# Moving the third batch's loads ahead of the second pass's W1, and the first batch's beta split behind the fourth pair's q

## The chip, the cores and the metric

The kernel runs on one core of a Trainium2 chip. The metric is the device time of one execution in microseconds (us), lower is better. One execution was also taken with the hardware profiler; all rows below come from it.

## The reference

For each of 8 batches, grouped-query attention runs over 384 positions (16 query heads, 4 key/value heads, head size 64), and its result, laid out as 384 x 1024, goes through an affine token-mixing and channel-mixing block:

```python
attn = softmax(q @ k.T / sqrt(64)) @ v        # per head; 4 q heads share a k, v head
x    = attn.transpose(0, 2, 1, 3).reshape(8, 384, 1024)
a1   = alpha1 * x + beta1
u    = x + lam * einsum('ts,bsd->btd', w_tok, a1)
a2   = alpha2 * u + beta2
out  = u + lam * (relu(a2 @ w_ch1) @ w_ch2)   # w_ch1 1024 x 4096, w_ch2 4096 x 1024
```

## The kernel before, in words

`main(b)` is the channel mixing of batch b and is called a pass here; there are eight. Its first half is `h` (line 407): 32 groups of 8 matmuls each, whose 256-column tiles of W1 come from HBM again in every pass through a ring of five (`load_w1`, line 128, on the POOL queue). Its second half is `ch` (line 441): two column halves times three row blocks, each 32 matmuls against W2, which is loaded once, during the first pass, and stays (`load_w2`, line 133, POOL queue).

`side(b)` is the attention and token mixing of batch b. For batches 1 to 7 its steps are woven, one at a time, between the matmuls of the pass before: `main(b)` yields after each four matmuls, and the loop at the end of the kernel compares the work done (`t` against `t_all`) with the share of steps issued. For the first batch no pass is there to hide it: its steps run alone at the start, in an order written out by hand (the dictionary `at`: after the scores of step i, the listed functions are issued). Every engine takes its instructions in the order in which these functions issue them.

The functions that matter at the start, with their lines: `scores` (202, exponent on ACT at 211), `av_piece` (237 on PE; then on DVE reciprocal 242, x 243, product with alpha1 247), `q_transpose` (188, copied out at 190), `k_transpose` (177, 179), `wtok_transpose` (297, copied out on DVE at 300), `rows_r` (307 and 311 on PE, 314 on ACT, 315 to 317 on DVE), `tok` (259, 263; DVE 266). In batch 0 lam is folded into alpha1 and beta1, and beta enters as one more product of rank 32 (line 263): `scale_rows(1)` (519) multiplies the beta1 rows by lam, `split(1, 2)` (527, 528, 527, 528, 531) writes them as a sum of bf16 rows in `rows_b`, `fill_h` (535) spreads them into `H`, and `tok` needs `H` and `R` (from `rows_r`). Buffers of PSUM are shared by tags: `av`, one of the q transposes and `tok` of batch 0 take turns in the two buffers of the tag `mm`; `wtok_transpose` and others in the one buffer each of `av` and `tp`.

The loads of batch b+2 happen in pass b: `load_k` at its start on the SP queue, later `place_k` (four casts on POOL, line 101), `load_q` (110) and `load_v` (105) on the POOL queue, and then `flip_k` and `flip_q` (113, 117), two DMA transposes on the SP queue, which also carries the stores of `out` (448) and the transposes of `a2` (282). In the first pass the POOL queue also holds, at the end of `h`, the five W1 tiles of the second pass.

Of the kernel before, what the change touches and what calls it, by code (L numbers as in the profile page):

```python
# [12 lines left out]
def kernel(  # L13
# [29 lines left out]
    B, Hq, S, D = q.shape  # L43
# [37 lines left out]
    def by_st(ap):  # L81
        return ap.rearrange("h (p st) d -> p st h d", st=NST)
# [3 lines left out]
    def load_k(b, hs=(0, 2)):  # L86
        ks.setdefault(b, [])
        for h in hs:
            t = sb.tile([P, 2, NST, D], f32, tag="kst", name="kst", bufs=2)
            nc.sync.dma_start(out=t, in_=k[b, h:h + 2].rearrange("h (p st) d -> p h st d", st=NST))  # L90
            ks[b].append(t)

    def place_k(b, i, hs=(0, 1)):
        if b not in k2s:
            k2s[b] = sb.tile([P, NST, Hkv, 2, D], bf, tag="k2", name="k2", bufs=1)
        copies = [nc.gpsimd.tensor_copy] * 2
        if b == 1 or b == 0 == i:
            copies = (nc.vector.tensor_copy, nc.vector.tensor_copy if i else nc.scalar.copy)
        lo, hi = hs[0], hs[-1] + 1
        for a in range(2):  # L100
            copies[a](out=k2s[b][:, :, 2 * i + lo:2 * i + hi, a, :], in_=ks[b][i][:, lo:hi].rearrange("p h st d -> p st h d"))

    def load_v(b, sts=range(NST)):
        for st in sts:
            nc.gpsimd.dma_start(out=vt[b % 2][:, st, :, :D], in_=by_st(v[b])[:, st])

    def load_q(b):
        qrs[b] = sb.tile([P, Hq, NST, D], bf, tag="q_raw", name="q_raw", bufs=1)
        for h in range(0, Hq, G):
            nc.gpsimd.dma_start(out=qrs[b][:, h:h + G], in_=q[b, h:h + G].rearrange("h (p st) d -> p h st d", st=NST))  # L110

    def flip_k(b):
        nc.sync.dma_start_transpose(out=kT.rearrange("p st h s -> p (st h) s"),
                                    in_=k2s[b].rearrange("p st h a d -> p (st h a d)"))

    def flip_q(b):
        nc.sync.dma_start_transpose(out=qT.rearrange("p a j s -> p (a j) s"),
                                    in_=qrs[b].rearrange("p h st d -> p (h st d)"))
# [5 lines left out]
    def load_w1(n):  # L124
        if n < B * NCH:
            t = sb.tile([P, NDT, CW * P], bf, tag="w1", name="w1", bufs=RING)
            c = n % NCH
            nc.gpsimd.dma_start(out=t, in_=w1src[:, :, c * CW * P:(c + 1) * CW * P])  # L128
            w1_tiles[n] = t

    def load_w2(dw, i, n):
        r, cs = slice(i * NNT // n, (i + 1) * NNT // n), slice(dw * 512, (dw + 1) * 512)
        nc.gpsimd.dma_start(out=w2[:, r, cs], in_=w2src[:, r, cs])
# [6 lines left out]
    def evac(eng):  # L140
        return nc.scalar.copy if eng == "ACT" else nc.vector.tensor_copy
# [16 lines left out]
    def side(b):  # L158
# [173 lines left out]
        def add(f, *a):  # L332
            us.append(lambda: f(*a))
# [35 lines left out]
        lower, upper = range(NP // 2), range(NP // 2, NP)  # L369
        def av(p):  # L370
# [2 lines left out]

        ut = a2_transpose
        at = {0: [(warmup, 3), (scale_rows, 0), (split, 0, 1, 0)], 1: [(k_transpose, 1, 1), (split, 0, 1, 1)],
              2: [(q_transpose, 2, 2, "av")], 3: [(warmup, 1), (spread, lower, (0, 1), "tp"), (scale_rows, 1), (split, 1, 2, 0)],
              4: [(split, 1, 2, 1), (av, 0)], 5: [(wtok_transpose, 0, "av"), (wtok_transpose, 1, "tp")],
              6: [(av, 1), (wtok_transpose, 2, "av"), (k_transpose, 2, 2, "tp")], 7: [(q_transpose, 4, 2, "av"), (fill_h, 0)],
              8: [(rows_r, "tp"), (av, 2)], 9: [(spread, upper, (0, 1), "av", "ACT"), (q_transpose, 6, 2, "mm")],
              10: [(tok, 0)],  # L380
              11: [(av, 3)], 12: [(tok, 1), (ut, 0)], 13: [(av, 4), (tok, 2)], 14: [(ut, 1), (fill_h, 4), (tok, 3)],
              15: [(av, 5), (ut, 2)], 16: [(tok, 4), (ut, 3)], 17: [(av, 6), (tok, 5)]}
# [4 lines left out]
        for f, *a in ((ut, 4), (h_part, (0, 1), range(4)), (av, 7), (ut, 5), (tok, 6),  # L387
                      (h_part, (2, 3), range(4)), (h_part, range(4), (4,)), (ut, 6), (tok, 7),
                      (h_part, range(4), (5,)), (ut, 7), (h_part, range(4), (6,)), (h_part, range(4), (7,))):
            add(f, *a)  # L390
        return us


    T_H, T_C = 4 * S, 4 * 512

    def main(b):
        a2T = a2Ts[b % 2]
        x = xs.pop(b)
        n = S + 1 if b == 0 else S
        for c in range(NCH):  # L400
            w1 = w1_tiles.pop(b * NCH + c)
            for j in range(CW):
                nt = c * CW + j
                begun = b == 0 and nt in early
                ps = early[nt] if begun else psum.tile([P, 512], f32, tag="mm", name="h", bufs=2)
                for dt in range(0 if begun else NDT):
                    nc.tensor.matmul(out=ps[:, :n], lhsT=w1[:, dt, j * P:(j + 1) * P],  # L407
                                     rhs=a2T[:, dt, :n], start=(dt == 0), stop=(dt == NDT - 1))
                    if dt == 3:
                        yield T_H  # L410
                c1 = bias1[:, nt:nt + 1]
                if b == 0:
                    evac("DVE" if nt % 2 else "ACT")(out=c1, in_=ps[:, S:n])
                if nt % 2 == 0:
                    nc.scalar.activation(out=hT[:, nt, :], in_=ps[:, :S], func=RELU, bias=c1)  # L415
                else:
                    nc.vector.tensor_scalar(out=hT[:, nt, :], in0=ps[:, :S], scalar1=c1,  # L417
                                            scalar2=0.0, op0=ADD, op1=mybir.AluOpType.max)
                yield T_H

            if b or c + RING < NCH:
                load_w1(b * NCH + c + RING)
            if b == 0 and c in (3, 5, 7, 9):
                load_w2(0, 8 + c // 2 - 1, 16)
            if b == 0 and c == NCH - RING:
                for i in (6, 7):
                    load_w2(0, i, 8)
                for i in range(8):
                    load_w2(1, i, 8)
            if b == 0 and c == NCH - 1:  # L430
                for i in range(RING):
                    load_w1(NCH + i)
        for dw in range(NDW):
            cs = slice(dw * 512, (dw + 1) * 512)
            for ms in range(NST):
                ps = psum.tile([P, 512], f32, tag="mm", name="ch", bufs=2)
                o = sb.tile([P, 512], f32, tag="tmp", name="o", bufs=4)
                last = (b, dw, ms) == (B - 1, NDW - 1, NST - 1)
                for lo, hi in ((0, 256), (256, 384), (384, 512)) if last else ((0, 512),):
                    for nt in range(NNT):  # L440
                        nc.tensor.matmul(out=ps[:, lo:hi], lhsT=hT[:, nt, ms * P:(ms + 1) * P],  # L441
                                         rhs=w2[:, nt, dw * 512 + lo:dw * 512 + hi], start=(nt == 0), stop=(nt == NNT - 1))
                        if nt % 4 == 3 and nt < NNT - 1:
                            yield T_C
                    c = slice(dw * 512 + lo, dw * 512 + hi)
                    nc.vector.tensor_tensor(out=o[:, lo:hi], in0=ps[:, lo:hi], in1=lam_t[:, c], op=MUL)  # L446
                    nc.vector.tensor_tensor(out=o[:, lo:hi], in0=o[:, lo:hi], in1=x[:, ms, c], op=ADD)  # L447
                    nc.sync.dma_start(out=out[b].rearrange("(p st) d -> p st d", st=NST)[:, ms, c], in_=o[:, lo:hi])
                yield T_C

    t_all = 2 * NNT * T_H + 8 * NST * NDW * T_C
    order = {mybir.EngineType.PE, mybir.EngineType.DVE, mybir.EngineType.Activation,
             mybir.EngineType.Pool, mybir.EngineType.SP}
    with tc.manual_schedule(engines=order):
# [97 lines left out]
        for f in side(0):  # L552
            f()
        place_k(1, 0)
        place_k(1, 1)
        for b in range(B):
            us = side(b + 1) if b + 1 < B else []
            half = False
            done, t, loaded, flipped = 0, 0, b + 2 >= B, b + 2 >= B
            lead, span = (0.04, 0.82) if b == 0 else (0, 0.95)  # L560
            if not loaded:
                load_k(b + 2)
            for dt in main(b):
                t += dt
                half = not half
                if late and half:
                    late.pop(0)()
                if done < len(us) and done * t_all * span < len(us) * (t - t_all * lead):
                    us[done]()
                    done += 1  # L570
                if not loaded and t > t_all * 0.55:
                    loaded = True
                    place_k(b + 2, 0)
                    place_k(b + 2, 1)
                    load_q(b + 2)
                    load_v(b + 2)
                if not flipped and t > t_all * 0.85:
                    flipped = True
                    flip_k(b + 2)
                    flip_q(b + 2)  # L580
            while done < len(us):
                us[done]()
                done += 1
# [30 lines left out]
```

## Time and profile before

| | |
|---|---|
| median of 6 runs | 813.1 us (812.38 to 814.86) |
| the profiled execution | 813.11 us, of it span 811.0 us |
| PE busy | 800.7 us (99% of the span) |
| DVE, ACT, POOL busy | 344.4, 225.9, 178.1 us |
| mean granted TensorE clock | 0.998 |
| bytes | 112.96 MB in DMA packets, mean 139 GB/s |
| first batch's attention alone | until about 41.7 us |
| first pass, `h` then `ch` | to 88.9 us, then to 138.5 us |
| each later pass but the last | 97.45 us |

Busy times are unions of an engine's instructions; matmuls overlap one another, so the mean duration of one is longer than its share of the time. A number in square brackets at the end of a timeline row is the time that the engine sat idle before it, and who ended it.

### The profile page before, as it was taken

What the parts mean: (1) busy time and instruction counts of PE and PEld (TensorE: products, weight loads), DVE (VectorE), ACT (ScalarE), POOL (GpSimd) and SP (SyncE); (2) the same over time, 40 slices, a digit from 0 to 9 for tenths busy, and PEclk for the clock granted to TensorE, in tenths of its full rate; (3) what the DMA queues carried; (4) which work ended last, traced back from release to release, by engine and by line L of the source; (5) the groups of instructions that cost most, each with busy time, mean ns of one, the idle gap of its engine ahead of it and who ended that gap; (6) DMA issues with size and microseconds to landing.
All of it is one profiled execution on the core that took longest, in us unless ns stands there. A gap on an engine that the chain in (4) does not pass through costs nothing.

```text
span 811.0 us, 14160 instructions
## 1 busy us (share of the span) xinstructions
PE 800.7 (99%) x6129; PEld 450.7 (56%) x6129; DVE 344.4 (42%) x669; ACT 225.9 (28%) x311; POOL 178.1 (22%) x232
## 2 busy tenths in 40 slices
PE   7999999999999999999999999999999999999997
PEld 4766555665556655566455655556555565556545
DVE  7745543244433444344452445434444344432122
ACT  5654311332113311233103331034211432102100
POOL 7135230334003230133202240022500321003000
PEclk9999999999999999999999999999999999999999
DMA  9999999999179992799848998499935998129611
GB/s 191 198 185 200 204 206 180 172 173 169 37 141 176 170 152 66 135 173 172 115 100 133 179 171 88 108 142 166 190 64 109 156 177 116 39 66 185 86 40 40
DMA packets 233550, 112.96 MB, mean 139 GB/s; under 512 B 82952, under 2 KB 227344, under 8 KB 233488
## 3 DMA queue, kind: packets, MB, share of 16 engines
q0 software_dynamic: 170736, 83.47, 83.7%
q1 hardware_dynamic: 62208, 28.20, 14.7%
q8 instruction: 48, 0.79, 0.4%
q10 hardware_dynamic: 544, 0.39, 0.1%
q14 instruction: 14, 0.11, 0.1%
HBM read 170.53 MB, written 12.58 MB: 226 GB/s over the span
## 4 chain that ended last, share of the span: by engine, by line
PE 95%; DVE 4%; issue 0%; ACT 0%; DVEq 0%
PE ch L441 41%; PE h L407 39%; PE av L237 4%; PE sc L202 4%; PE tok L259 4%; DVE hT L417 1%; DVE x L243 1%; PE h L152 1%; DVE a1f L250 0%; DVE a L252 0%; PE warm L459 0%; PE tp L188 0%; PE ut L276 0%; DVE hT L528 0%; PE vec L325 0%
## 5 line engine op out<-in xcount | busy, mean ns | idle before, releaser
L441 PE MATMUL ch<-w,hT 128*128 128x512 bf16 (+2 forms) x1600 | 353.4, 371 | 0.9 <-DVE o L446 0.9
L407 PE MATMUL h<-a2T,w 128*128 128x384 bf16 (+1 forms) x2016 | 349.5, 326 | 0.9 <-DVE hT L417 0.3
L407 PEld LDWEIGHTS <-w 128*128 128x128 bf16 x2016 | 189.4, 98 | 125.5 <-issue 8.7
L441 PEld LDWEIGHTS <-hT 128*128 128x128 bf16 x1600 | 146.3, 98 | 154.2 <-issue 5.8
L128 POOL DMA_DIRECT2D w<-in_moe_w_ch_dram x128 | 112.6, 882 | 541.1 <-PE h L407 493.7
L211 ACT ACTIVATE es<-sc 128x1024 bf16<-128x1024 f32 x126 | 123.4, 1021 | 289.2 <-PE sc L202 289.2
L417 DVE TENSOR_SCALAR hT<-h,bias 128x384 bf16<-128x384 f32 x128 | 79.0, 618 | 187.0 <-PE h L407 186.4
L415 ACT ACTIVATE hT<-h,bias 128x384 bf16<-128x384 f32 x128 | 74.3, 581 | 202.9 <-PE h L407 202.4
L446 DVE TENSOR_TENSOR o<-ch,vecs 128x512 f32<-128x512 f32 (+2 forms) x50 | 33.3, 667 | 91.1 <-PE ch L441 91.1
L266 DVE TENSOR_TENSOR x<-tok,x 128x384 f32<-128x384 f32 x64 | 35.6, 555 | 80.5 <-PE tok L259 78.3
L237 PEld LDWEIGHTS <-es 128*128 128x128 bf16 x1008 | 45.8, 97 | 20.5
L237 PE MATMUL av<-v,es 128*128 128x65 bf16 x1008 | 49.0, 193 | 0.0
L202 PE MATMUL sc<-qT,kT 64*128 64x384 bf16 (+2 forms) x576 | 46.0, 274 | 0.1
L259 PEld LDWEIGHTS <-wtokT 128*128 128x128 bf16 x576 | 37.8, 98 | 12.4 <-issue 0.4
L242 DVE RECIPROCAL rinv<-av 128x6 f32<-128x6 f32 x64 | 12.3, 193 | 71.1 <-PE av L237 70.8
L259 PE MATMUL tok<-a,wtokT 128*128 128x128 bf16 x504 | 37.3, 219 | 0.0
L243 DVE TENSOR_TENSOR x<-av,rinv 128x384 f32<-128x384 f32 x64 | 35.7, 557 | 2.2
L202 PEld LDWEIGHTS <-kT 64*128 64x128 bf16 x576 | 20.0, 94 | 28.1 <-issue 23.7
L447 DVE TENSOR_TENSOR o<-o,x 128x512 f32<-128x512 f32 (+2 forms) x50 | 33.5, 671 | 1.7
L270 DVE TENSOR_TENSOR a<-x,vecs 128x384 bf16<-128x384 f32 x56 | 31.4, 561 | 1.9
L252 DVE TENSOR_TENSOR a<-a1f,vecs 128x384 bf16<-128x384 f32 x56 | 31.2, 558 | 2.2
L250 DVE TENSOR_TENSOR a1f<-x,vecs 128x384 f32<-128x384 f32 x56 | 31.2, 558 | 1.9
(75 smaller groups left out, 198.5 us busy)
## 6 DMA issues: line engine op xcount, KB each, us to landing
w<-in_moe_w_ch_dram POOLq DMA_DIRECT2D x138, 512.0 KB, 7.9
out_dram<-o SPq DMA_DIRECT2D x47, 256.0 KB, 2.3
q_raw<-in_q_dram POOLq DMA_DIRECT2D x28, 192.0 KB, 7.0
kst<-in_k_dram SPq DMA_DIRECT2D x16, 192.0 KB, 3.2
w<-in_moe_w_ch_dram POOLq DMA_DIRECT2D x1, 2048.0 KB, 15.8
v<-in_v_dram POOLq DMA_DIRECT2D x24, 64.0 KB, 6.8
w<-in_moe_w_ch_dram POOLq DMA_DIRECT2D x4, 256.0 KB, 8.3
a2T<-a SPq DMA_TRANSPOSE x54, 2.3
```

The source lines that it names most:

```text
L128: nc.gpsimd.dma_start(out=t, in_=w1src[:, :, c * CW * P:(c + 1) * CW * P])
L202: nc.tensor.matmul(out=sc[:, hh, k % 4:k % 4 + n], lhsT=kT[r, sk, 2 * p // G, :], rhs=qT[r, p, st:st + n, :], start=True, stop=True)
L211: nc.scalar.activation(out=e, in_=sc, func=EXP, scale=scale_qk)
L237: nc.tensor.matmul(out=av[:, hh, sq, :], lhsT=ess[k // 4][:, m % 2, k % 4, :], rhs=vb[:, sk, hk, :], start=(sk == 0), stop=(sk == NST - 1))
L243: nc.vector.tensor_tensor(out=x[:, :, cols(p)].rearrange("p st (h d) -> p h st d", h=2), in0=av[:, :, :, :D], in1=rinv.to_broadcast([P, 2, ...
L259: nc.tensor.matmul(out=ps[:, tt, :], lhsT=wtokT[:, st, tt * P:(tt + 1) * P], rhs=a1s[p][:, st, :], start=(st == 0), stop=(st == NST - 1 an ...
L266: nc.vector.tensor_tensor(out=u, in0=ps, in1=u, op=ADD)
L407: nc.tensor.matmul(out=ps[:, :n], lhsT=w1[:, dt, j * P:(j + 1) * P], rhs=a2T[:, dt, :n], start=(dt == 0), stop=(dt == NDT - 1))
L415: nc.scalar.activation(out=hT[:, nt, :], in_=ps[:, :S], func=RELU, bias=c1)
L417: nc.vector.tensor_scalar(out=hT[:, nt, :], in0=ps[:, :S], scalar1=c1, scalar2=0.0, op0=ADD, op1=mybir.AluOpType.max)
L441: nc.tensor.matmul(out=ps[:, lo:hi], lhsT=hT[:, nt, ms * P:(ms + 1) * P], rhs=w2[:, nt, dw * 512 + lo:dw * 512 + hi], start=(nt == 0), sto ...
L447: nc.vector.tensor_tensor(out=o[:, lo:hi], in0=o[:, lo:hi], in1=x[:, ms, c], op=ADD)
```

## The change

Four edits. First, in the hand-written order of batch 0, `scale_rows(1)` goes from step 3 and the two halves of `split(1, 2)` from steps 3 and 4 to step 7, behind the q transpose of the fifth and sixth pairs; `fill_h(0)` goes from step 7 to step 8. On DVE this puts six instructions behind the copies of the first two pairs, of w_tok, k and q, and ahead of `fill_h`. Second, `place_k`, `load_q` and `load_v` of a batch become `load_next`. Third, in the first pass `load_next(2)` is called at the end of `h`, ahead of the five W1 loads, where before it came at 55% of the pass, behind them. Fourth, the two flips of the first pass are issued at 75% in place of 85%. Later passes keep their places. PE and ACT issue the same instructions in the same order; on SP the two flips go ahead of one store and one transpose of `a2`.

```diff
-  3: [(warmup, 1), (spread, lower, (0, 1), "tp"), (scale_rows, 1), (split, 1, 2, 0)],
-  4: [(split, 1, 2, 1), (av, 0)], 5: [(wtok_transpose, 0, "av"), (wtok_transpose, 1, "tp")],
-  6: [(av, 1), (wtok_transpose, 2, "av"), (k_transpose, 2, 2, "tp")], 7: [(q_transpose, 4, 2, "av"), (fill_h, 0)],
-  8: [(rows_r, "tp"), (av, 2)], 9: [(spread, upper, (0, 1), "av", "ACT"), (q_transpose, 6, 2, "mm")],
+  3: [(warmup, 1), (spread, lower, (0, 1), "tp")],
+  4: [(av, 0)], 5: [(wtok_transpose, 0, "av"), (wtok_transpose, 1, "tp")],
+  6: [(av, 1), (wtok_transpose, 2, "av"), (k_transpose, 2, 2, "tp")], 7: [(q_transpose, 4, 2, "av"), (scale_rows, 1), (split, 1, 2)],
+  8: [(fill_h, 0), (rows_r, "tp"), (av, 2)], 9: [(spread, upper, (0, 1), "av", "ACT"), (q_transpose, 6, 2, "mm")],
...
+    def load_next(b):
+        place_k(b, 0)
+        place_k(b, 1)
+        load_q(b)
+        load_v(b)
...
             if b == 0 and c == NCH - 1:
+                load_next(2)
                 for i in range(RING):
                     load_w1(NCH + i)
...
-            done, t, loaded, flipped = 0, 0, b + 2 >= B, b + 2 >= B
+            done, t, loaded, flipped = 0, 0, b == 0 or b + 2 >= B, b + 2 >= B
...
-            if not loaded:
+            if b + 2 < B:
                 load_k(b + 2)
...
                 if not loaded and t > t_all * 0.55:
                     loaded = True
-                    place_k(b + 2, 0)
-                    place_k(b + 2, 1)
-                    load_q(b + 2)
-                    load_v(b + 2)
-                if not flipped and t > t_all * 0.85:
+                    load_next(b + 2)
+                if not flipped and t > t_all * (0.85 if b else 0.75):
```

More of the change, by code (lines that the diff above doesn't have):

```diff
@@ L375, in side @@
         at = {0: [(warmup, 3), (scale_rows, 0), (split, 0, 1, 0)], 1: [(k_transpose, 1, 1), (split, 0, 1, 1)],
-              2: [(q_transpose, 2, 2, "av")], 3: [(warmup, 1), (spread, lower, (0, 1), "tp"), (scale_rows, 1), (split, 1, 2, 0)],
-              4: [(split, 1, 2, 1), (av, 0)], 5: [(wtok_transpose, 0, "av"), (wtok_transpose, 1, "tp")],
-              6: [(av, 1), (wtok_transpose, 2, "av"), (k_transpose, 2, 2, "tp")], 7: [(q_transpose, 4, 2, "av"), (fill_h, 0)],
-              8: [(rows_r, "tp"), (av, 2)], 9: [(spread, upper, (0, 1), "av", "ACT"), (q_transpose, 6, 2, "mm")],
+              2: [(q_transpose, 2, 2, "av")], 3: [(warmup, 1), (spread, lower, (0, 1), "tp")],
+              4: [(av, 0)], 5: [(wtok_transpose, 0, "av"), (wtok_transpose, 1, "tp")],
+              6: [(av, 1), (wtok_transpose, 2, "av"), (k_transpose, 2, 2, "tp")], 7: [(q_transpose, 4, 2, "av"), (scale_rows, 1), (split, 1, 2)],
+              8: [(fill_h, 0), (rows_r, "tp"), (av, 2)], 9: [(spread, upper, (0, 1), "av", "ACT"), (q_transpose, 6, 2, "mm")],
               10: [(tok, 0)],
```

## The prediction

> **What bounds the kernel now.** I read the page first, for the engine that has no idle time to give away.
>
> ```profile
> span 811.0 us, 14160 instructions
> PE 800.7 (99%) x6129; PEld 450.7 (56%) x6129; DVE 344.4 (42%) x669; ACT 225.9 (28%) x311; POOL 178.1 (22%) x232
> ```
>
> PE idles 10.3 us in all. About 0.9 us of it are PE's two short gaps inside the last output tile (from 802.8), some 3 us the last results' way out, 1.5 us the start. The timeline of PE shows the rest in one place:
>
> ```profile
> 12.38 0.72 PE L237 MATMUL av<-v,hT 128*128 128x65 bf16 x18
> 15.50 0.33 PE L297 MATMUL tp<-ident,stage 128*128 128x128 bf16 x3 [2.41 <-DVE wtokT L300]
> 15.77 0.49 PE L177 MATMUL tp<-ident,k 128*128 128x128 bf16 x6
> 16.19 0.39 PE L202 MATMUL sc<-qT,kT 64*128 64x256 bf16 x4
> 17.32 0.80 PE L188 MATMUL tp<-ident,qg 128*128 128x128 bf16 x6 [0.73 <-DVE wtokT L300]
> ...
> 22.24 0.34 PE L259 MATMUL tok<-hT,wtokT 128*128 128x128 bf16 x3
> ```
>
> Two stalls, 2.41 and 0.73 us, both for DVE's copies of the turned w_tok. The timeline of DVE tells why the copies are late:
>
> ```profile
> 11.00 0.27 DVE L519 TENSOR_TENSOR hT<-hT 32x128 f32<-32x128 f32 x1
> 11.30 0.27 DVE L527 CAST hT<-hT 32x128 bf16<-32x128 f32 x1
> 11.61 1.03 DVE L528 SCALAR_TENSOR_TENSOR hT<-hT,stage 32x128 f32<-32x128 bf16 x1
> 12.67 0.55 DVE L527 CAST hT<-hT 32x128 bf16<-32x128 f32 x1
> 13.26 0.34 DVE L528 SCALAR_TENSOR_TENSOR hT<-hT,stage 32x128 f32<-32x128 bf16 x1
> 13.64 0.33 DVE L531 CAST hT<-hT 32x128 bf16<-32x128 f32 x1
> 13.78 0.19 DVE L242 RECIPROCAL rinv<-av 128x6 f32<-128x6 f32 x1
> ...
> 15.10 0.61 DVE L300 COPY wtokT<-tp 128x384 bf16<-128x384 bf16 x2
> ...
> 18.63 0.67 DVE L535 TENSOR_TENSOR stage<-hT,stage 32x512 bf16<-32x512 bf16 x1
> 20.58 0.60 DVE L315 SCALAR_TENSOR_TENSOR stage<-hT,stage,r 32x384 bf16<-32x384 bf16 x1 [1.28 <-ACT hT L314]
> ```
>
> The first six rows are beta's scale and split; the copies stand behind them. Later DVE itself waits 1.28 us. The table by stretches (its columns: stretch, length, busy time and count of PE, PEld, DVE, ACT, POOL, then the granted clock) shows what the stalls cost next:
>
> ```profile
> 10.42:13.84 3.42, 2.67 (x54) 1.90 (x52) 3.25 (x8) 3.23 (x4) 3.42 (x7) 1.00 1.48 202
> 13.84:17.25 3.41, 1.08 (x13) 0.73 (x13) 3.25 (x11) 0.56 (x1) 1.57 (x3) 1.00 1.39 209
> 17.25:20.66 3.41, 3.34 (x28) 1.92 (x28) 1.71 (x5) 1.95 (x3) 0.69 (x1) 0.50 1.43 202
> ```
>
> PE was busy 1.08 of 3.41 us, and the next 3.41 us ran at half clock. From 17.3 to 802.8 us the chain of waits is PE but for small pieces, so what PE gains before 22 us should reach the end.
>
> **The change part by part.** Sums are against the profiled execution, 813.11 us (span 811.0 and 2.1 around it), which equals the median of 813.1.
>
> *The six instructions leave their place.* The products that the 13.78 reciprocal reads end at 11.35 (a row at 10.63 lasting 0.72), so it can start at 11.38, 2.40 earlier. All that follows on DVE up to the second w_tok copy and the copy of k keeps its spacing: the products at 12.38 end by 13.1, in time for the second reciprocal (15.63 becomes 13.23). PE's two stalled rows then start at 13.10 and 14.92. The q row's transposes take about 0.43 until the next row (0.73 at half clock), and DVE's copy of that q starts near 15.5.
>
> *They come back behind it.* By start to start, the first split (6.84 to 9.82, its gap left out), under POOL's DMA issues, gives 2.25; the least rows of each kind (0.30, 0.25, 0.37, 0.28, 0.37, 0.33) give 1.9; the removed block itself took 2.78, with POOL's casts beside it. Ends 1.75 and 2.78; I take 2.05, as POOL then has one DMA issue (16.31), no cast. From 15.95 the block runs to 18.0. `fill_h` delays line 315 by 0.6, to 18.6. ACT's copy for it is no longer late: PE's rows of line 307 follow at about 15.7, and ACT is free from about 16.8. From line 315 to the end of the third pair's x it is 1.44 (20.58 to 22.02), so 20.04. `tok` needs that buffer: 20.1 for 22.24, **2.1 us earlier** (2.4 to 1.4 by the block's ends). PE waits there from 18.5, about 1.6 us. The next av needs the last q copy, 1.6 after that x starts, 21.15 for 23.34: the gain holds. ACT's exponents, 1.02 each, had waits of 3.04, 1.05 and 0.87 here and stay ahead.
>
> *What was covered by the later start.* PE arrives earlier everywhere; DMA does not. The sixth W1 tile, issued at 41.88, lands after 6.7, at 48.6; PE uses it at 51.8 (16 products a tile, counted from 41.75), so 3.2 us are left and its issue, which waits for PE, moves along. The turned q of batch 2 was near: issued on SP at 131.61, 5.8 to landing by the page's median, 137.4, for scores at 139.10. With PE 2 us earlier it would be 0.3 late; the moved flips end this.
>
> *The third batch's loads.* Four POOL casts (1.86), four q and three v issues (0.74 each, 5.2) go ahead of five W1 issues (0.88 each). All seven DMAs and five tiles stand in one queue, so the last lands no earlier or later: in the profile the last W2 piece lands at 110.3 (issued 87.38, 22.9 on), W1 at 126.3, v at 134.9. With q and v first (8.6 us as there), they land by 119, the first W1 near 122 and the fifth near 135. PE wants the first at 136.5: 14 us of cover; the other four are wanted some 3 us apart. Cost 0.
>
> *The flips.* SP gets to them after the a2 transpose (117.26 less 2, and 1.24): 3.39 and 4.37 put the store and a2 transpose behind them near 124.4, some 0.7 later than they would be. That transpose feeds the second pass near 137; its slowest like ones took 7 to 8 us. Waits for PE's last scores (114.4 less 2) and for the q landing (about 115) are over by then. Cost 0; if they were late, the a2 transpose and two stores would be queued behind.
>
> *The casts beside DVE.*
>
> ```profile
> 102.24 1.86 POOL L101 CAST k<-kst 128x384 bf16<-128x384 f32 x4
> ```
>
> They had DVE to themselves. Now they follow the W2 issue of 87.38, at 88.1 to 90.0, and lines 250 and 252 (0.56 each, at 90.24 and 90.84 before) come at 88.2 and 88.8. Line 528 at 11.61, beside two such casts, took 1.03 for 0.34. If both wait for the last cast, `a` ends near 91.1 for 89.4; `tok` wants it at 90.2: **0 to 0.95 lost, I take 0.2**, since the gaps in DMA after 41 us close with PE's earlier issues, which brings the W2 landings, and so the casts, forward.
>
> [...]
>
> **Sum:** 813.1 - 2.1 + 0.2 = **811.2 us**.
>
> **The rivals.**
>
> *Half clock again* (0.16). The new 1.6 us wait leaves PE busy 1.7 to 2.0 us of some 3.41 us stretch. 1.08 halved the clock, 2.67 did not; also at the start 2.07 of 3.42 (0.18 to 3.60) did not lift it, for the products of 128x384 are 0.34 apart until about 7 us. If halved, a full stretch of PE loses about 1.4 (av 0.95 for 0.65, scores 0.54 for 0.33): 812.6. Against it: where the stretches begin may differ, and only half the positions hold the whole wait.
>
> [...]
>
> *Casts in full* (0.08): 0.95 for 0.2, 812.0.
>
> *Hidden* (0.05): the block costs DVE as much before `tok` as it frees: 813.1. It needs 4.2 us where the block ever took 2.78.
>
> *W1 late, slower* (0.09). q and v delay the second pass's first tile past 136.5: that needs 14 us more than the 8.6 that the seven loads took. A wait of POOL on a landing could do it, each tile standing behind the one before; beyond it every us is paid by PE. From 16 us on it is slower than before; at 20, 815.2. The W2 issues' waits of 2 to 3 us each at 81 to 90 us speak against so much.
>
> **How the numbers follow.** The forecast has 0.62, with its own range 810.5 to 811.9 from the block's and the casts' ends. About 0.2% (1.63 us) is what can be told from no change; four fifths of the forecast's chance lies beyond it: faster 0.50. The remaining 0.12 and the half clock, casts and hidden cases make 0.41 for the same; slower 0.09. The range, 810.5 to 813.2, leaves out W1 late and a little below.
>
> **What the new profile would show.** PE's stalls for line 300 below 0.9 together; one wait ahead of the first `tok`, which starts near 20.1; granted clock 1.00 in 17.25 to 20.66, and the following stretch decides the first rival. `ch` starts near 87 for 88.9, the second pass near 136.6 for 138.5, with 97.45 from there per pass. A PE wait at about 90 is the casts; a PE wait on a W1 tile or on the turned q near 137 refutes the load steps. The forecast is wrong if DVE's moved block takes over 2.5 us or PE runs at half clock after 20 us.

## The result and the profile after

The changed kernel takes 811.3 us (median; 810.6 to 813.57) against 813.12 for the kernel before run beside it: a ratio of 0.9981, 95% interval 0.9975 to 0.9988. The change makes it 0.19% faster, 1.5 us by the ratio. The profiled execution took 811.46 us, its span 809.3 (before 813.11 and 811.0).

The page of the changed kernel:

```profile
span 809.3 us, 14160 instructions
PE 799.3 (99%) x6129; PEld 450.2 (56%) x6129; DVE 343.3 (42%) x669; ACT 225.9 (28%) x311; POOL 178.4 (22%) x232
```

PE, in order of time, at the start:

```profile
11.80 0.72 PE L237 MATMUL av<-v,hT 128*128 128x65 bf16 x18
12.78 0.33 PE L297 MATMUL tp<-ident,stage 128*128 128x128 bf16 x3 [0.26 <-DVE wtokT L300]
...
14.60 0.49 PE L188 MATMUL tp<-ident,qg 128*128 128x128 bf16 x6 [0.73 <-DVE wtokT L300]
...
19.51 0.34 PE L259 MATMUL tok<-hT,wtokT 128*128 128x128 bf16 x3 [1.31 <-DVE x L243]
```

The stall of 2.41 us is 0.26, the one of 0.73 has stayed, and a wait of 1.31 stands ahead of the first `tok`. DVE, with the six moved instructions at their new place (lines 526 and 534 to 538 are the former 519 and 527 to 531):

```profile
15.13 0.56 DVE L190 COPY qT<-tp 128x768 bf16<-128x768 bf16 x1
15.61 0.27 DVE L526 TENSOR_TENSOR hT<-hT 32x128 f32<-32x128 f32 x1
15.91 0.21 DVE L534 CAST hT<-hT 32x128 bf16<-32x128 f32 x1
16.16 0.34 DVE L535 SCALAR_TENSOR_TENSOR hT<-hT,stage 32x128 f32<-32x128 bf16 x1
...
17.16 0.21 DVE L538 CAST hT<-hT 32x128 bf16<-32x128 f32 x1
17.41 0.68 DVE L542 TENSOR_TENSOR stage<-hT,stage 32x512 bf16<-32x512 bf16 x1
18.02 0.59 DVE L315 SCALAR_TENSOR_TENSOR stage<-hT,stage,r 32x384 bf16<-32x384 bf16 x1
```

The block takes 1.80 us (15.61 to 17.41), and line 315 no longer waits for ACT. In the table by stretches (stretch, length, busy time and count of PE, PEld, DVE, ACT and POOL, granted clock, two columns on DMA) the clock is whole:

```profile
13.84:17.25 3.41, 2.67 (x41) 1.71 (x40) 3.12 (x10) 2.40 (x3) 1.93 (x3) 1.00 1.42 205
17.25:20.66 3.41, 2.10 (x32) 1.40 (x32) 3.31 (x10) 2.43 (x3) 0.59 (x1) 1.00 1.42 207
```

Then something that was not there before, at the turn from the first pass to the second. SP's queue first, then PE:

```profile
115.87 4.13 SPq L113 DMA_TRANSPOSE kT<-k  x1
120.19 13.09 SPq L117 DMA_TRANSPOSE qT<-q_raw  x1
133.37 0.53 SPq L455 DMA_DIRECT2D out_dram<-o  x1
133.95 1.51 SPq L282 DMA_TRANSPOSE a2T<-a  x1
```

```profile
135.63 0.81 PE L413 MATMUL h<-a2T,w 128*128 128x384 bf16 x4
137.06 0.61 PE L202 MATMUL sc<-qT,kT 64*128 64x384 bf16 x8 [0.61 <-DMA qT<-q_raw]
```

The q flip holds SP for 13.09 us where it held it for 4.37, and PE waits for the turned q. So the time was gained at the start and partly given back at the turn. The table splits the profiled executions at four rows of PE: the first av, the first `tok`, the first `h` of the second pass, and the end of the span.

| | first av | first tok | from av to tok | second pass | from there to the end |
|---|---|---|---|---|---|
| before | 10.63 | 22.24 | 11.61 | 138.35 | 672.67 |
| changed | 9.97 | 19.51 | 9.54 | 135.63 | 673.66 |

From the first `tok` to the second pass both take 116.1 us. The first `tok` came 2.73 earlier: 0.66 because the first av did, 2.07 after it. The 0.66 is no part of the change, since no instruction ahead of the first av has moved on any engine; that row lies between 9.65 and 10.73 in the profiles of all these kernels. At the turn 0.99 was lost, which leaves 1.74.

### The profile page after: what moved, and what is told of

The parts are those of the page before. It is cut to its first block, busy times and chain, and to the rows that moved or that the text cites. A ratio compares the mean times of both kernels' runs of the same rounds, so it can differ in the third digit from the quotient of the medians.

```text
span 809.3 us, 14160 instructions
## 1 busy us (share of the span) xinstructions
PE 799.3 (99%) x6129; PEld 450.2 (56%) x6129; DVE 343.3 (42%) x669; ACT 225.9 (28%) x311; POOL 178.4 (22%) x232
## 4 chain that ended last, share of the span: by engine, by line
PE 85%; DMA 9%; DVE 4%; issue 1%; POOL 1%; ACT 0%; SPq 0%; POOLq 0%; DVEq 0%
PE ch L448 36%; PE h L413 36%; DMA w<-in_moe_w_ch_dram 6%; PE av L237 4%; PE sc L202 4%; PE tok L259 4%; DMA q_raw<-in_q_dram 2%; DVE x L243 1%; DVE hT L423 1%; PE h L152 1%; DMA a2T<-a 1%; DVE a1f L250 0%; DVE a L252 0%; POOL w L133 0%; PE warm L466 0%
```

## The experiments

Two theories stood at first. A: DVE's queue sets the start, and the loss at the turn comes from running the flips beside the second pass's W1 tiles. B, the prediction's: the moved loads and flips cost nothing and are needed once the start is faster. Later runs asked what share the half clock had, and whether DVE's queue still sets the start. The medians of a group of runs have spans by themselves, so where the parts of the run are in question, the segments of the table are compared.

**The start alone.** The new order of batch 0 in the kernel before, nothing else:

```diff
--- before
+++ e1
-  3: [(warmup, 1), (spread, lower, (0, 1), "tp"), (scale_rows, 1), (split, 1, 2, 0)], 4: [(split, 1, 2, 1), (av, 0)],
+  3: [(warmup, 1), (spread, lower, (0, 1), "tp")], 4: [(av, 0)],
-  7: [(q_transpose, 4, 2, "av"), (fill_h, 0)], 8: [(rows_r, "tp"), (av, 2)],
+  7: [(q_transpose, 4, 2, "av"), (scale_rows, 1), (split, 1, 2)], 8: [(fill_h, 0), (rows_r, "tp"), (av, 2)],
```

> Only the beta split is moved; the third batch's loads and the flips stay where they were. In the changed kernel the first pass's ch began 2.72 us earlier, and 0.74 was lost at the turn to the second pass, where PE waited for the turned q, whose flip took 13.09 us of SP in place of 4.37. Theory A (the flip is slow because it runs beside W1 tiles): here the q loads come last, the flips run when W1 has landed, the q flip takes 4 to 6 us and the scores wait 0 to 0.4; the whole is 0.3 to 0.7 us faster than the changed kernel, near 810.8, and 2.1 to 2.4 faster than before. Theory B (the prediction's: without the moved loads and flips the turned q would be late by what PE gained): PE waits 0.3 to 1.0 at the turn, and the time is that of the changed kernel or a little more, 811.3 to 812.0.

Measured: 810.93 us, ratio 0.9967 (0.9955 to 0.9979). From av to tok 9.25, from the second pass on 672.82: 0.15 lost at the turn, a visible wait of 0.08. The q flip:

```profile
125.00 3.37 SPq L113 DMA_TRANSPOSE kT<-k  x1
131.08 4.22 SPq L117 DMA_TRANSPOSE qT<-q_raw  x1
```

So the start alone has all of the gain. The turned q is just about late, as the prediction feared, but by 0.1 and not by 0.3 or more: in this run the last W2 piece landed at 108.6 and the last q at 130.9, against 110.3 and 131.4 before, because W1's issues follow PE (in the profile of before POOL waits 493.7 us for `h` ahead of them) and came earlier.

**The loads and flips alone.** The changed kernel with the order of batch 0 of before.

```diff
--- changed
+++ e2
-  3: [(warmup, 1), (spread, lower, (0, 1), "tp")],
+  3: [(warmup, 1), (spread, lower, (0, 1), "tp"), (scale_rows, 1), (split, 1, 2, 0)],
...
```

> Only the loads and the flips are moved; the start is that of before. Theory A: the start is as before (stalls of about 2.4 and 0.7 us for line 300), and the q flip takes 10 us or more beside W1, so that it lands near 138 to 139.5, when PE arrives for scores at 139: 0 to 0.6 lost, 813.1 to 813.8. Theory B (moved loads and flips are harmless or useful by themselves): 812.8 to 813.2, with a q flip that lands well before 137.

Measured: 813.15 us, ratio 1.0004 (0.9992 to 1.0016), no change.

```profile
121.97 12.34 SPq L117 DMA_TRANSPOSE qT<-q_raw  x1
```

PE comes to the scores at 138.46 and does not wait, 672.68 from the second pass on. The slow flip is there, and the later start covers it. This run also shows how much one execution's start can be off: with the order of before and with half clock after the stall, it takes 10.87 from av to tok where before took 11.61. Its six instructions lasted 2.07 (11.12 to 13.19) where those of before lasted 2.78; POOL's casts began at 11.44 in both, and why the six were quicker here is not shown.

**The flips back at 85%.**

```diff
--- changed
+++ e3
-                if not flipped and t > t_all * (0.85 if b else 0.75):
+                if not flipped and t > t_all * 0.85:
```

> The changed kernel with the flips back at 85% of the first pass. Theory A (what hurts is that flips and W1 share the time): the flips start near 124, W1 lands until about 135, so the q flip ends later than in the changed kernel, and PE waits 1 to 4 us at the turn: 812 to 815. Rival (what hurts is the early place of the flips alone): the q flip takes about 4.4 us and there is no wait: 810.6.

Measured: 810.59 us, ratio 0.9964 (0.9952 to 0.9976). The time is the rival's, but not by its mechanism, and theory A's wait of 1 to 4 us did not come. The flip and the scores:

```profile
127.41 6.67 SPq L117 DMA_TRANSPOSE qT<-q_raw  x1
```

```profile
136.25 0.61 PE L202 MATMUL sc<-qT,kT 64*128 64x384 bf16 x8 [0.48 <-DMA qT<-q_raw]
```

It is 673.23 from the second pass on, 0.56 lost. Started 7 us later, the flip has less W1 beside it (the last tiles landed at 128.5 and 132.8) and ends nearly at the same time, 134.1 for 133.3. Nothing here shows a gain from 75%.

**W1 behind the flips.** Three of the five W1 tiles get a one-column copy on POOL that reads the turned q, so that their loads wait for the flips; the load then overwrites the column.

```diff
--- changed
+++ e4
+    def load_w1(n, after=None):
...
+            if after is not None:
+                nc.gpsimd.tensor_copy(out=t[:, 0, :1], in_=after)
...
-                for i in range(RING):
+                for i in range(2):
                     load_w1(NCH + i)
...
                     flip_q(b + 2)
+                    for i in range(2, RING if b == 0 else 2):
+                        load_w1(NCH + i, qT[:, 7, 2, :1])
```

> The changed kernel, but three of the second pass's five W1 tiles wait (by a one-column copy on POOL that reads the turned q) until the flips have landed. Theory A: the q flip takes 4 to 6 us, the wait of 0.61 at the turn and the 0.13 behind it are gone, and the three tiles land by 137, before PE wants them (142 on): 0.7 faster than the changed kernel, near 810.6. Rival (the flip is slow by the q landings or by the a2 transposes around it, not by W1): the flip takes more than 10 us still and the time stays at 811.3.

Measured: 810.83 us, ratio 0.9966 (0.9954 to 0.9978). SP's queue and PE at the turn:

```profile
116.32 3.39 SPq L113 DMA_TRANSPOSE kT<-k  x1
119.90 5.11 SPq L117 DMA_TRANSPOSE qT<-q_raw  x1
125.11 0.53 SPq L457 DMA_DIRECT2D out_dram<-o  x1
```

```profile
136.07 0.81 PE L415 MATMUL h<-a2T,w 128*128 128x384 bf16 x4
136.82 0.61 PE L204 MATMUL sc<-qT,kT 64*128 64x384 bf16 x8
```

With only W1's place changed, the flip falls from 13.09 to 5.11 us, the wait is gone, and it is 672.67 from the second pass on, as before the change. The three tiles landed at 134.3, 138.8 and 141.4, later than the 137 expected, but PE wants the third tile only near 142 and the others some 3 us apart, and nothing waited. This shows that W1 beside the flips is what made them slow.

**Half clock or DVE's queue.** The kernel before, with the second pair's av products issued four times:

```diff
--- before
+++ e5
-            for sq in range(NST):
+            for sq in list(range(NST)) * (4 if first and p == 1 else 1):
```

> The kernel before, with the second pair's av products issued four times over (each time from a fresh start, so the result stays): PE is busy from 13.0 to about 15.0, where it waited 2.41 us, and DVE's work is the same. It asks what share of the start's gain came from the half clock of 17.25 to 20.66. Theory A (DVE's queue sets the start; the half clock only made ACT's and so DVE's line 315 late by 1.28): the clock stays at 1.00, and from the first av to the first tok it takes 10.2 to 10.9 us (before 11.60, changed kernel 9.54): 812.0 to 812.6. Rival (the half clock was the whole gain): 9.5, 811.0. Rival (it was none of it): 11.4 to 11.6, 813.

Measured: 811.37 us, ratio 0.998 (0.9972 to 0.9989), as fast as the changed kernel, by work that is thrown away. From av to tok 10.60, inside theory A's bounds: DVE's copies of w_tok come as late as before (PE still waits until 15.48), but the stretch after is not at half clock, and line 315's wait falls from 1.28 to 0.65:

```profile
13.84:17.25 3.41, 1.85 (x39) 1.42 (x36) 3.25 (x11) 0.58 (x1) 1.56 (x3) 1.00 1.39 210
17.25:20.66 3.41, 3.36 (x51) 2.23 (x50) 2.60 (x8) 2.47 (x4) 0.68 (x1) 1.00 1.44 201
```

So of the 2.07 us between the first av and `tok`, about 1.0 is the half clock that the stall brought, and the rest DVE's queue (the six instructions took 2.86 in this run, about as long as the 2.78 of before, so the two profiles can be compared; by e2, 0.7 of that rest is how long they happened to take in the profile of before). The median gained more than the 1.0 of the profile, 1.6 us by the ratio. The runs' mean granted clocks point to why: half clock for one stretch of 3.41 us takes 0.002 off the mean (the profile of before has one, 17.25 to 20.66, and a mean of 0.998); of the 24 runs of before in this comparison 7 stood at 0.998, one stretch, and 17 at 0.995 to 0.997, more than one (their medians are 811.9 and 813.7), while all 11 of this kernel stood at 0.999 or 1.000. The profiled execution of before was one of those that lost least.

**DVE's gaps filled.** In the kernel of e4, beta's scale and the first half of its split go where DVE waited for PE:

```diff
--- e4
+++ e6
-  0: [(warmup, 3), (scale_rows, 0), (split, 0, 1, 0)],
+  0: [(warmup, 3), (scale_rows, 0), (split, 0, 1, 0), (scale_rows, 1)],
-  3: [(warmup, 1), (spread, lower, (0, 1), "tp")],
+  3: [(warmup, 1), (spread, lower, (0, 1), "tp"), (split, 1, 2, 0)],
-  7: [(q_transpose, 4, 2, "av"), (scale_rows, 1), (split, 1, 2)],
+  7: [(q_transpose, 4, 2, "av"), (split, 1, 2, 1)],
```

> The kernel of e4 (changed start, three W1 tiles behind the flips), but beta's scale goes to step 0 and the first half of its split to the end of step 3, where DVE waits 0.45 and 0.38 us for PE; only the second half of the split stays behind the fifth pair's q. Theory A (after the change DVE's queue still sets the start; PE waits 1.31 for the first tok): from the first av to the first tok 0.6 to 0.8 less than in e4's 9.33, the wait for tok near 0.6, 810.2. Rival (the wait for tok is not DVE's queue but PE's or ACT's work for the third pair): 9.2 to 9.4, 810.8.

Measured: 811.06 us (809.54 to 811.84), ratio 0.9972 (0.9961 to 0.9983). From av to tok 8.71, 0.62 less than e4, and the wait ahead of `tok` is 0.49 where it was 1.30:

```profile
18.69 0.34 PE L261 MATMUL tok<-hT,wtokT 128*128 128x128 bf16 x3 [0.49 <-DVE x L245]
```

DVE's queue does set the start after the change. The profiled execution took 809.54; the median was above the 810.2 that was expected, and by the ratio e6 is no faster than e4 (0.9972 for 0.9966).

**The changed kernel again, twice, and the two starts beside it.** e7 and e8 are the changed kernel, e9 is e6, and e10 is e6's order of batch 0 in the kernel before.

> The changed kernel once more beside the two others, on the same chip, for the comparison and for a second look at its start and its turn: from the first av to the first tok 9.2 to 9.6 us, a q flip of 10 us or more, a wait of 0.4 to 0.8 for the turned q at the turn, 811.3.

> The changed kernel a third time, beside the two others. So far its runs lie in two groups, near 810.8 and near 812.4, at the same granted clock. Theory A (the turned q lands at about 137 whatever PE does, so that an early start is lost again in a wait at the turn, and a late landing is the second group): the profile shows the rest of the run from the second pass on at 672.67 where PE reaches the turn's scores after about 136.8, and longer by what it comes earlier: first tok plus 789.0 is 808.7 at the least. Rival (the groups come from the start, by the phase of the clock): the rest is 672.7 whatever the start.

> The kernel of e6 again. Theory A: with three W1 tiles behind the flips the turned q lands by 131, there is no wait at the turn, 672.67 from the second pass on, and no group near 812.4; the median is 0.6 to 1.0 below the changed kernel's, 810.4 to 811.0. Rival: the same spread as the changed kernel, since it comes from the start.

> The start of e6 with the loads and flips of the kernel before. Theory A (the turned q's landing is a floor set by the DMA queue, near 136.8 to 137.0 in e1): the 0.6 that the start gains over e1 are waited for at the turn, 673.2 to 673.6 from the second pass on, 810.9 as e1. Rival (DMA follows PE, as its W1 issues do): no wait, 810.3.

Measured: e7 811.70 (ratio 0.9983), e8 812.01 (0.9984, interval 0.9975 to 0.9993), e9 810.44 (0.9959, 0.9946 to 0.9972), e10 811.24 (0.9974, 0.9963 to 0.9985), above both of the times expected for it.

| | first tok | scores at the turn | waited there | from the second pass on |
|---|---|---|---|---|
| changed, e7 | 19.94 | 136.80 | 0 | 672.67 |
| changed, first profile | 19.51 | 137.06 | 0.61 | 673.66 |
| changed, e8 | 19.17 | 137.55 | 1.45 | 674.46 |
| e4 | 19.95 | 136.82 | 0 | 672.67 |
| e6 | 18.69 | 135.55 | 0 | 672.66 |

The row of PE in e8:

```profile
137.55 0.61 PE L202 MATMUL sc<-qT,kT 64*128 64x384 bf16 x8 [1.45 <-DMA qT<-q_raw]
```

The flip took 13.11 and 13.28 us in e7 and e8. In the changed kernel the earlier PE arrives, the more it waits, and a landing half a microsecond later adds to that: e8 began 0.34 us earlier than the first profile and ended 0.45 later. Theory A's floor of about 808.7 holds for these three spans (808.7, 809.3, 809.7); e6, without W1 beside the flips, ended at 807.5. e7's expected wait of 0.4 to 0.8 did not come, as its start was late enough. No profile fell among the slower executions of the changed kernel: at full clock, those of e7 lie at 810.8 to 811.0 and again at 812.4 to 812.8, while those of e1, e3 and e4 (five or six each) end at 811.5. That the second group comes from W1 beside the flips is not shown, for e10, with the flips in their old place, has one execution at 812.34.

e10 tells nothing on the floor: its profiled execution, like e9's, had its first `tok` at 20.0, and both arrived late at the turn. What happened there is the half clock, in the new start this time. The table of e9, then the same of e6:

```profile
12.49:15.90 3.41, 1.94 (x24) 1.27 (x24) 3.22 (x9) 1.71 (x2) 2.73 (x4) 1.00 1.45 200
15.90:19.32 3.42, 3.42 (x33) 2.15 (x33) 3.12 (x11) 1.88 (x3) 0.19 (x1) 0.50 1.38 213
```

```profile
12.49:15.90 3.41, 2.39 (x26) 1.37 (x25) 3.19 (x10) 2.11 (x3) 2.64 (x5) 1.00 1.45 200
15.90:19.32 3.42, 2.93 (x51) 2.23 (x50) 3.28 (x10) 3.00 (x5) 0.63 (x1) 1.00 1.39 214
```

The same program, the same order; PE busy 1.94 of 3.41 us in one execution and 2.39 in the other, and only the first lost its clock: 10.11 from av to tok for 8.71. In e9 the first pair's product with alpha1 (line 249 there, 247 before), beside POOL's casts, took 1.10 for 0.66, so the copies of w_tok came 0.45 later and PE waited 0.79 for them, not 0.32. The stretches of e6 also began 0.6 later than those of e9; counted from there, its two were busy 2.68 and 2.92.

The version with both repairs has the shortest profile (e6) and the lowest ratio (e9): beside e8's 0.9984, it stands at 0.9959 of the kernel before. But e6, the same kernel, stands at 0.9972, and the ratios of e1, e3 and e4 (0.9967, 0.9964, 0.9966) lie inside e9's interval, so that it is faster than these is not shown.

## Why the prediction was right, point by point

The time was forecast at 811.2 and is 811.3, faster by 0.19%, just inside what was called no change; that case had been given 0.41, and a gain beyond it 0.50. That the number came so close is in part luck. In the two profiles the terms are 2.07 gained for 2.1, 0 lost for 0.2 at the casts, and 0.99 lost for 0 at the flips: 1.08 in all for 1.9. The profiled execution still ended near the forecast because its first av happened to come 0.66 earlier; for the median's part see the end of this section.

- *The six instructions leave their place.* Right: the first reciprocal came at 10.72 for 13.78, 3.06 earlier, of which 0.66 is the first av's; that leaves the 2.40. The w_tok copies gained less, 2.06 (12.38 for 15.10, less 0.66), because line 247 took 0.91 for 0.56 beside POOL's casts, a delay that the working had not counted. PE's two stalls together are 1.0, where "below 0.9" was named.
- *They come back behind it.* Right: the block took 1.80 for 2.05, inside 1.75 to 2.78; the wait for `tok` was 1.31 for 1.6; from the first av to `tok` 2.07 were gained for 2.1, as the shorter block made up most of line 247's delay. e1 shows the same gain without the rest of the change (11.61 to 9.25). Against e2, whose start is also that of before, the changed kernel's first profile gains 1.33; that 2.1 was met so closely depends on the profile of before.
- *The casts beside DVE.* 0.2 taken, 0 measured. The prediction put them at 88.1 to 90.0 and said that earlier W2 landings would pull them forward; they came at 85.81 to 87.67, and line 250 began at 87.52 with 0.57. What a DVE row loses beside the casts was thus hardly put to the test there; in the start the product of line 247 at 11.54, beside the casts of 11.48 to 12.82, took 0.91 for 0.56.
- *The third batch's loads.* The DMA order was as worked out: q and v by 114.7 (119 in the working), the fifth W1 tile at 135.6 (135), and PE waited for no tile. W1 late, the slower rival, did not come. (Its example was added up wrongly: with every us beyond 14 paid by PE, 20 us make 817.2 and not 815.2.) But the step charged the flips nothing for their company.
- *The flips* is the step that failed. It took 3.39 and 4.37 us of SP from the rows of before and called the cost 0. Those rows were of flips that ran when W1 had landed. Beside W1 the q flip took 13.09 to 13.28, SP reached the a2 transpose at 133.95 and not near 124.4, and the turn cost 0, 0.99 and 1.79 in three profiles. e4 shows the cause. The sentence on what a late flip would hold up (the a2 transpose and the stores) was right: the a2 transpose came 9.5 us later than it was put.
- *What was covered by the later start.* The turned q was near with the old loads, but e1 lost 0.15 there and not 0.3, and the moved flips did not end it: they made it worse.
- *Half clock again* did not come at the start in the changed kernel's profiles, where the stretch of the wait had 2.10 us busy (the first profile). In e9's and e10's start it came, behind 1.94 and 1.73 us, and six of the changed kernel's 44 executions, at a mean clock of 0.997 or 0.998, may have had it.

Two errors went against each other in the median: no charge for the flips, and a kernel before whose usual run, by its mean clock, loses more to half clock than its profiled one.

## What to carry to other kernels

A duration from a row holds for the company that the row had (the q flip took 4.37 us behind W1 and 13.09 beside it): before a DMA is moved, look at what its queue and the 16 engines carry at the new place, and price it by a row from there. PE's stall of 2.41 us cost twice here, once as the wait and once as the half clock behind it; filling the wait with any work showed the share of the half clock, about 1.0 us. When a step gains at the start, look for the next landing downstream that does not move with it: here it took gain back where there was most (no wait with the first `tok` at 19.94, 1.45 us with it at 19.17), and the runs lay wider apart (810.87 to 814.75 us in e8, 810.38 to 811.29 in e4).

## What the runs showed of the hardware that was not expected

- The clock fell without a long wait. In the profile of before it rose at 7.01, fell at 17.25 and rose again at 20.66, three and four steps of 3.41 us after the first rise. Of the stretches at the start, counted in such steps in each execution, those with 1.08, 1.38 (e2), 1.73 (e10) and 1.94 us (e9) of busy PE were followed by half clock; those with 2.06 (e5) and 2.10 us were not. No wait in e9's stretch was longer than 0.79 us. The stall in the profile of before had been 2.41. These rows are few, and of one kernel.
- Busy time alone does not decide it either. In e8, 134.38 to 137.79 had 1.96 us busy, hardly more than e9's stretch, and full clock after it; at the end of e2, 805.47 to 808.88 had 1.50 us busy, all of it products of 128x128 for the last output tile, and the clock stayed whole to the end of the span. What else counts is left open.
- Where the stretches lie differs from one execution to the next: the clock first rose at 4.5 to 7.0 us in the twelve profiles. The first `tok` of the changed kernel lay at 19.17, 19.51 and 19.94 in three. The rise alone does not order these (e5 has the rise at 4.6 and the first av at 10.53); what else moves the first av is left open.
- The q flip lost more beside W1's copies than the copies did beside it: it took 3.0 times as long (13.09 us for 4.37), while in the changed kernel the last three of the five W1 tiles landed 4.0 to 4.5 us apart, for 2.6 to 2.8 around 50 us, where no flip ran.
